# Decode attention over two key-value caches: the transposes of the small cache's first probabilities moved from in front of its second unit to behind that unit's second pair of steps

## The chip, the core and the metric

The kernel runs on one core of one Trainium2 chip. The metric is device time in microseconds (us), lower is better.

Names used below: PE is the tensor engine, PEld its weight load, DVE the vector engine, ACT the scalar engine, SP the sync engine, which only issues the large loads.

## The reference, cut to what matters

Two decode attentions for a single query position, 32 query heads of 128 each, in bf16. Cache A ("large") has 32 key-value heads with all of its 32768 positions in use. Cache B ("small") has 8 key-value heads, each shared by 4 query heads, and only the last 4096 positions count.

```python
q = (x @ wq).reshape(B, Sq, 32, 128).transpose(0, 2, 1, 3)      # x: [1, 1, 512]
scores = einsum("bhqd,bhkd->bhqk", q, k_cache) * 128 ** -0.5   # B: the last 4096 keys only
p = softmax(scores, axis=-1)
o = einsum("bhqk,bhkd->bhqd", p, v_cache)
out = o.transpose(0, 2, 1, 3).reshape(B, Sq, 32 * 128) @ wo    # A's and B's outputs side by side
```

Nearly all of the work is reading: about 570 MB of keys, values and weights.

## The kernel before

The program is a list of operations per engine, in program order, with semaphores placed from the dependencies. The parts that matter (cuts marked `...`):

```python
def plan(self):
    ...
    self.load_wq("B")                        # v buffer 0
    for g in range(2):
        self.load_kv("k", "B", g, 0, 0)      # k buffers 0 and 1
    self.load_wq("A")                        # v buffer 1
    self.emit_qproj("B")
    self.emit_unit("B", 0, 0, 0)             # transposes of K, copies out of PSUM, scores
    self.emit_stats("B", 0, 0)               # max, exponential -> psb
    self.emit_PT("B", 0, 0)                  # transposes of psb -> ptsb
    self.emit_unit("B", 1, 0, 0, lambda: self.emit_qproj("A"))
    self.emit_stats("B", 1, 0)
    for g in range(2):
        if g == 1:
            self.emit_PT("B", g, 0)
        self.load_kv("v", "B", g, 0, 0)      # v buffers 0 and 1
        self.emit_PV("B", g, 0, 0)
        self.emit_gather("B", g, 0)
    ...
    for i in range(self.NIT):                # the large cache: 32 rounds, 4 loads of 4 MB each
        ...

def emit_unit(self, name, g, r, u, late=None):
    slot = u if name == "A" else g
    for pr in range(4):                      # four pairs of steps
        for st in (2 * pr, 2 * pr + 1):
            for half in range(2):
                self.emit_T(slot, st, half)  # 8 transposes into one of 4 PSUM banks, one copy on DVE
        if pr == 3 and late:
            late()                           # the large cache's q projection
        self.pending.append((name, g, r, u, pr, self.nbatch - 4))
        if len(self.pending) > 1:
            self.emit_S(self.pending.pop(0)) # scores of the pair before
```

First, there are two V buffers. The projection weights of the large cache (`wq` of A, 4 MB) sit in V buffer 1, and the small cache's second V load goes into the same buffer. So that load waits until PE has finished the large cache's q projection. Its semaphore comes with the first step of scores (four matmuls) after the projection. Second, SP issues its loads strictly in order, so every load of the large cache queues behind this one. PE in turn reaches the projection only after the last transposes of the second small-cache unit.

## Time and profile before

| | before |
|---|---|
| time, median of 3 runs | 1338.75 us (1337.97 to 1339.37) |
| span in the profile | 1335.2 us |
| PE / DVE busy | 71% / 59% |
| DMA over the span | 427 GB/s |
| second V load of the small cache issued at | 54.59 us |

From the page of the kernel before, part 1 (busy microseconds and share of the span) and part 2 (40 equal slices of the span; busy tenths of the DMA engines, then GB/s):

```profile
span 1335.2 us, 41413 instructions
PE 954.6 (71%) x19416; PEld 771.0 (58%) x19416; DVE 791.1 (59%) x1662; ACT 61.1 (5%) x201; POOL 2.0 (0%) x15
DMA  9999999999999999999999999999999999999998
GB/s 394 377 427 436 426 436 426 438 425 438 426 437 427 436 428 434 430 434 429 435 429 435 428 435 429 435 429 434 430 432 432 432 432 431 432 432 432 431 433 354
```

DMA moves at least 425 GB/s in all slices but three: the first (start), the last (end), and the second (33 to 67 us, 377 GB/s). The second is the one that can be repaired. The view of windows of 1 us shows it closely. Its columns are the window and its length, busy us and instruction count of each engine, the granted PE clock, the DMA share, and GB/s:

```profile
51.00:52.00 1.00, 1.00 (x46) 1.00 (x43) 1.00 (x3) 0.00 (x0) 0.00 (x0) 1.00 0.83 344
52.00:53.00 1.00, 1.00 (x46) 1.00 (x43) 0.23 (x1) 0.00 (x0) 0.00 (x0) 1.00 0.32 123
53.00:54.00 1.00, 1.00 (x46) 1.00 (x43) 0.00 (x0) 0.00 (x0) 0.00 (x0) 1.00 0.08 33
54.00:55.00 1.00, 1.00 (x21) 0.52 (x21) 0.19 (x1) 0.00 (x0) 0.00 (x0) 0.76 0.00 0
55.00:56.00 1.00, 1.00 (x16) 0.40 (x12) 0.24 (x1) 0.00 (x0) 0.00 (x0) 0.50 0.56 66
56.00:57.00 1.00, 1.00 (x16) 0.39 (x12) 0.90 (x4) 0.00 (x0) 0.00 (x0) 0.50 0.56 213
57.00:58.00 1.00, 1.00 (x13) 0.31 (x8) 0.91 (x5) 0.00 (x0) 0.00 (x0) 0.53 1.04 442
```

The last column falls to zero although PE is busy throughout: the load before has landed in full at 54.06 us and the next is not yet issued, so the queue holds nothing. The timeline says why (start, duration, engine, line, operation; in brackets the idle time before it and what ended that):

```profile
36.14 0.69 DVE L511 TENSOR_REDUCE tr_in<-psS 128x1 f32<-128x512 f32 x1 [0.51 <-PE psS L493]
...
39.47 0.69 ACT L525 ACTIVATE psb<-psS,nb_B 128x512 bf16<-128x512 f32 x1 [36.49 <-DVE nb_B L524]
...
40.31 0.61 PE L538 MATMUL psPT<-ident,psb 128*128 128x128 bf16 x4 [4.22 <-ACT psb L525]
40.71 5.45 PE L470 MATMUL psT<-ident,kbuf 128*128 128x128 bf16 x64
41.81 0.69 DVE L473 COPY kt<-psT 128x1024 bf16<-128x1024 bf16 x1 [2.37 <-PE psT L470]
...
50.87 3.34 PE L427 MATMUL psACC<-x_A,vbuf 128*128 128x1 bf16 x128
54.14 1.57 PE L493 MATMUL psS<-kt,qz 128*32 128x512 bf16 x16
...
54.59 0.37 SPq L291 DMA_DIRECT2D vbuf<-in_B_v_cache_dram  x1
```

Read it from the bottom. The V load is issued at 54.59, right after the projection (L427), which is the end of PE's second unit. That unit starts late. PE stands 4.22 us in front of the four transposes of psb (L538), because they need the exponential on ACT, which needs the statistics on DVE. Meanwhile the second unit's K data is there and four PSUM banks are free.

### The profile page before, as it was taken

The page shows a single profiled execution, that of the slowest core. Times are in us where ns is not written, and L with a number is a line of the kernel's source. Part 1 is how long each engine was busy: PE and PEld are TensorE (multiplying, and loading weights), DVE is VectorE, ACT ScalarE, POOL GpSimd, SP SyncE. Part 2 cuts the span into 40 slices and gives each one's busy share as a digit, 9 for nine tenths or more (in the row PEclk, how much of TensorE's full clock was granted, in tenths as well). Part 3 has the DMA queues.
Part 4 walks back from the last instruction along what each step waited for, and adds up shares of the span by engine and source line. Part 5 has one row for each costly group of instructions (what it writes and reads, how often), then busy time and mean ns, then how long its engine had stood idle before and what let it go on. Part 6 is the DMA issues. An engine that isn't in the chain of part 4 may idle for free.

```text
span 1335.2 us, 41413 instructions
## 1 busy us (share of the span) xinstructions
PE 954.6 (71%) x19416; PEld 771.0 (58%) x19416; DVE 791.1 (59%) x1662; ACT 61.1 (5%) x201; POOL 2.0 (0%) x15
## 2 busy tenths in 40 slices
PE   3676766877766787776767777666877766777776
PEld 3455555656655565665556566555655655566663
DVE  3564655676555576655556665555666555666652
ACT  0000000000000000000000000000000000000000
POOL 0000000000000000000000000000000000000000
PEclk9787888888787888887888888788889887888888
DMA  9999999999999999999999999999999999999998
GB/s 394 377 427 436 426 436 426 438 425 438 426 437 427 436 428 434 430 434 429 435 429 435 428 435 429 435 429 434 430 432 432 432 432 431 432 432 432 431 433 354
DMA packets 22003, 570.64 MB, mean 427 GB/s; under 512 B 2530, under 2 KB 2532, under 8 KB 2788
## 3 DMA queue, kind: packets, MB, share of 16 engines
q1 hardware_dynamic: 21700, 570.44, 99.5%
q8 instruction: 10, 0.16, 0.0%
q10 hardware_dynamic: 288, 0.00, 0.0%
q14 instruction: 5, 0.04, 0.0%
HBM read 570.43 MB, written 0.00 MB: 427 GB/s over the span
## 4 chain that ended last, share of the span: by engine, by line
DMA 64%; PE 26%; issue 0%; DVE 0%; SPq 0%
DMA kbuf<-in_A_k_cache_dram 63%; PE psT L470 22%; PE psS L493 4%; DMA kbuf<-in_A_wo_dram 2%; PE psPT L635 0%; DVE out_sb L639 0%; SPq L291 0%
## 5 line engine op out<-in xcount | busy, mean ns | idle before, releaser
L473 DVE COPY kt<-psT 128x1024 bf16<-128x1024 bf16 x1056 | 655.2, 684 | 216.8 <-PE psT L470 214.4
L470 PE MATMUL psT<-ident,kbuf 128*128 128x128 bf16 x8448 | 575.5, 233 | 138.3 <-DMA kbuf<-in_A_k_cache_dram 130.1
L470 PEld LDWEIGHTS psT<-ident,kbuf 128*128 128x128 bf16 x8448 | 536.2, 106 | 230.1 <-DMA kbuf<-in_A_k_cache_dram 138.2
L563 PE MATMUL psACC<-vbuf,ptsb 128*2 128x128 bf16 (+1 forms) x8256 | 188.5, 272 | 45.6 <-ACT ptsb L541 22.0
L563 PEld LDWEIGHTS psACC<-vbuf,ptsb 128*2 128x2 bf16 (+1 forms) x8256 | 169.0, 106 | 67.1 <-ACT ptsb L541 30.5
L493 PE MATMUL psS<-kt,qw 128*32 128x512 bf16 x2048 | 157.7, 385 | 15.2 <-DVE kt L473 15.2
L538 PE MATMUL psPT<-ident,psb 128*128 128x128 bf16 x136 | 20.5, 305 | 135.1 <-ACT psb L525 135.1
L592 DVE SCALAR_TENSOR_TENSOR oc_A<-psACC,hot_A,oc_A 128x128 f32<-128x128 f32 x48 | 16.8, 351 | 144.7 <-PE psACC L563 144.7
L538 PEld LDWEIGHTS psPT<-ident,psb 128*128 128x128 bf16 x136 | 11.6, 130 | 145.0 <-ACT psb L525 144.8
L525 ACT ACTIVATE psb<-psS,nb_A 128x512 bf16<-128x512 f32 x32 | 22.0, 687 | 1174.6 <-DVE nb_A L524 1174.6
L493 PEld LDWEIGHTS psS<-kt,qw 128*32 128x32 bf16 x2048 | 33.9, 95 | 57.7 <-DVE kt L473 31.0
L589 DVE TENSOR_SCALAR oc_A<-psACC,hot_A 128x128 f32<-128x128 f32 x16 | 5.6, 351 | 92.8 <-PE psACC L563 92.8
L511 DVE TENSOR_REDUCE tr_in<-psS 128x1 f32<-128x512 f32 x34 | 23.5, 692 | 18.1 <-PE psS L493 18.1
L606 PE MATMUL psG<-oc_A,hw 128*32 128x128 f32 (+1 forms) x128 | 14.4, 223 | 24.9 <-DVE oc_A L592 19.4
L514 DVE COPY m<-tr_a 1x16 f32<-1x16 f32 (+1 forms) x136 | 22.3, 164 | 2.6
L606 PEld LDWEIGHTS psG<-oc_A,hw 128*32 128x32 f32 x128 | 6.6, 110 | 29.9 <-issue 29.9
L520 DVE COPY b_A<-mr_A 1x16 f32<-1x16 f32 x128 | 21.2, 165 | 2.4
L541 ACT ACTIVATE ptsb<-psPT 128x512 bf16<-128x512 bf16 x34 | 20.3, 597 | 18.5 <-PE psPT L538 18.5
L575 DVE TENSOR_SCALAR oc_A<-oc_A,alpha_A 128x129 f32<-128x129 f32 x16 | 4.6, 290 | 16.4 <-ACT alpha_A L528 16.4
L427 PE MATMUL psACC<-x_B,vbuf 128*128 128x1 bf16 x128 | 3.6, 165 | 13.2 <-DMA vbuf<-in_B_wq_dram 13.2
L427 PEld LDWEIGHTS psACC<-x_B,vbuf 128*128 128x128 bf16 x128 | 3.5, 104 | 13.2 <-issue 13.2
L528 ACT ACTIVATE alpha_A<-cm_A,nb_A 128x1 f32<-128x1 f32 x32 | 9.0, 283 | 0.0
(71 smaller groups left out, 105.9 us busy)
## 6 DMA issues: line engine op xcount, KB each, us to landing
kbuf<-in_A_k_cache_dram SPq DMA_DIRECT2D x64, 4096.0 KB, 28.1
vbuf<-in_A_v_cache_dram SPq DMA_DIRECT2D x64, 4096.0 KB, 29.8
kbuf<-in_B_k_cache_dram SPq DMA_DIRECT2D x2, 4096.0 KB, 27.8
vbuf<-in_B_v_cache_dram SPq DMA_DIRECT2D x2, 4096.0 KB, 19.0
vbuf<-in_B_wq_dram SPq DMA_DIRECT2D x1, 4096.0 KB, 12.4
vbuf<-in_A_wq_dram SPq DMA_DIRECT2D x1, 4096.0 KB, 41.9
kbuf<-in_B_wo_dram SPq DMA_DIRECT2D x2, 2048.0 KB, 25.6
kbuf<-in_A_wo_dram SPq DMA_DIRECT2D x1, 1536.0 KB, 22.2
```

The costliest lines, as they stand in the source:

```text
L470: inst = e.transpose(T[:, 128 * k:128 * k + 128], src[:, DH * tile:DH * tile + DH], self.ident[:, :])
L473: self.copies.append(self.op("dve", lambda v: v.tensor_copy(KT[:, :], T[:, :]), o, to="pe"))
L493: inst = e.matmul(self.S[32 * c:32 * c + 32, :], lhsT=win, rhs=self.kt[(bb + c // 2) % NKT][:, 512 * (c % 2):512 * (c % 2) + 512], start=f ...
L511: o = dve(lambda v: v.reduce_max(tr["in"][:, 0:1], self.S[:, :], axis=AXX), self.sdone, self.k_pool)
L514: x = dve(lambda v, c=c: v.tensor_copy(m4[0:1, W * c:W * c + W], tr["a"][32 * c:32 * c + 1, 0:W]), o)
L520: x = dve(lambda v, c=c: v.tensor_copy(t["b"][32 * c:32 * c + 1, 0:W].rearrange("p (k h) -> p k h", k=KC), t["mr"][0:1, k, :].unsqueeze(1) ...
L525: self.sread = self.op("act", lambda s: s.activation(out=self.psb[:, :], in_=self.S[:, :], func=ACTF.Exp, bias=t["nb"][:, k:k + 1], scale= ...
L538: inst = e.transpose(PT[:, 128 * jj:128 * jj + 128], self.psb[:, 128 * jj:128 * jj + 128], self.ident[:, :])
L541: self.ptread = self.op("act", lambda s: s.activation(out=self.ptsb[:, :], in_=PT[:, 0:512], func=ACTF.Copy), self.psread, to="pe")
L563: inst = e.matmul(acc[32 * c:32 * c + HG, 0:w], lhsT=pt[:, col:col + HG], rhs=vv[:, :, 16 * kc + 4 * c + jj, :], start=(kc == 0 and jj == ...
L592: self.oop = dve(lambda v, src=src, hot=hot: v.scalar_tensor_tensor(out=oc, in0=src, scalar=hot, in1=oc, op0=ALU.mult, op1=ALU.add), pv, b ...
L606: self.gath = self.op("pe", lambda e, c=c, c2=c2: e.matmul(self.G[0:32, c0 + c:c0 + c2], lhsT=win, rhs=t["oc"][:, c:c2], start=False, stop ...
```

## The change

The intent is to give PE work while DVE and ACT prepare the first probabilities. The transposes of psb move behind the second unit's second pair of steps, where psb is ready. The single `late` hook becomes a table of hooks by pair.

```diff
         self.emit_stats("B", 0, 0)
-        self.emit_PT("B", 0, 0)
-        self.emit_unit("B", 1, 0, 0, lambda: self.emit_qproj("A"))
+        self.emit_unit("B", 1, 0, 0, {1: lambda: self.emit_PT("B", 0, 0), 3: lambda: self.emit_qproj("A")})
         self.emit_stats("B", 1, 0)
...
-    def emit_unit(self, name, g, r, u, late=None):
+    def emit_unit(self, name, g, r, u, hooks={}):
...
-            if pr == 3 and late:
-                late()
+            if pr in hooks:
+                hooks[pr]()
```

No instruction is added or removed. On PE, four matmuls change places with 64; the other engines keep their order.

## The prediction

> **What bounds the kernel.** DMA: the page gives 427 GB/s over the span, and the table of 20 us windows a DMA share of 0.99 to 1.03 from 100 us to 1320 us (PE is busy 71%, DVE 59%). A few microseconds on PE or DVE are worth something only where the DMA queue runs dry. Outside start and end, the 1 us windows show that once, from about 52 us (51:52 344 GB/s, 52:53 123, 53:54 33, 54:55 0, 55:56 66, 56:57 213, 57:58 442): against 430 GB/s, 4 to 4.5 us of lost transfer.
>
> **Why there.** SP issues in order. Its second small-cache V load waits for the large cache's q projection, which reads the same buffer (and for the score matmul after it, which carries the semaphore). The timeline has that projection at 50.87 to 54.21 us and the issue at 54.59; the next K loads queue behind it. So the end of the second small-cache unit's transposes on PE, which the projection follows, is on the critical path.
>
> **What the change moves.** No instruction is added or removed; PE's order shows only the four psb transposes moved, from before the second unit's first 64 transposes (8 groups) to after them. Before, PE finished the first unit's scores at 36.1, then waited 4.22 us for the exponential on ACT, which follows the statistics on DVE (36.14 to 39.43). DVE's copies out of PSUM began only at 41.81, the first of them every 0.85 us, bound by PE; later ones every 0.605. Now four transpose groups fill the four free PSUM banks during the statistics (by bytes moved, the K data landed near 34 us). DVE starts copying at 39.43, 2.4 us earlier. The fifth group still waits for the first copy (about 40.2), so PE idles about 2 us.
>
> **Clock.** The windows show the granted clock fall to 0.50 at about 37.5 us and return at about 44.3; transposes then take 107 ns instead of 56 ns. The Trainium skill, "TensorE: Matmul & The Clock Gate", Part 1 (the HAM clock gate), says that the clock halves after an idle window of about 3.4 us and returns after a busy one; the trace agrees roughly. Estimates from these durations: if PE is cold until 44.3 again, the second unit's transposes end near 48.9, 2 us sooner (the copies' 2.4 us less a bubble in which DVE waits for PE); if it stays warm, DVE's cadence rules and they end near 47.4, 3.5 us sooner. The moved transposes cost PE 0.4 us either way; their output is not needed before the V product near 52 us. Central: 2.4 us.
>
> **On the critical path.** All of it: the V load issue moves from 54.6 to about 52.2 us, the DMA gap shrinks from 4 to about 1.5 us, everything behind shifts by as much, and a saturated DMA neither gives it back nor adds to it. The gap caps the gain at about 4.
>
> **Prediction.** 1336.4 us, range 1334.8 to 1338.4. Faster by over 2%: 0.01; within 2%: 0.98; slower: 0.01.
>
> **What would show it.** PE's wait for the exponential gone from the second unit's head, replaced by a wait for DVE of about 2 us; first copy of unit two at 39.4; the large cache's projection ending at 50.7 to 52.2; second V issue 0.4 us later; more GB/s in 52 to 58 us; the loop's K loads all 2 to 3.5 us earlier.
>
> **What would make it wrong.** The large cache's projection weights landing after 47 us; the second K landing after 36; the loop absorbing the shift through slack that I don't see; a colder PE eating the gain; chip variation of 0.5 us hiding it.

## The result and the profile after

| | before | after |
|---|---|---|
| median, first measurement (4 runs each) | 1338.87 us | 1336.07 us (1335.95 to 1337.26) |
| ratio, 95% interval | | 0.9982 (0.9965 to 0.9999) |
| span in the profile | 1335.2 us | 1334.2 us |
| second small-cache V load issued | 54.59 us | 53.28 us |
| PE idle at the head of the second unit | 4.22 us | 2.11 us, after four groups |

The page of the kernel after, the same lines:

```profile
span 1334.2 us, 41413 instructions
PE 956.5 (72%) x19416; PEld 771.4 (58%) x19416; DVE 790.9 (59%) x1662; ACT 61.2 (5%) x201; POOL 2.0 (0%) x15
DMA  9999999999999999999999999999999999999998
GB/s 393 394 424 436 427 435 428 434 430 432 431 433 431 432 431 430 433 431 432 431 432 430 432 433 430 433 431 433 428 434 429 432 432 432 432 430 434 430 433 351
```

Busy times are within 2 us of before. What moved is the second slice, from 377 to 394 GB/s. The windows of 1 us of the kernel after:

```profile
51.00:52.00 1.00, 1.00 (x46) 1.00 (x44) 0.00 (x0) 0.00 (x0) 0.00 (x0) 1.00 0.90 360
52.00:53.00 1.00, 1.00 (x31) 0.74 (x32) 0.19 (x1) 0.00 (x0) 0.00 (x0) 0.67 0.26 107
53.00:54.00 1.00, 1.00 (x16) 0.32 (x8) 0.00 (x0) 0.00 (x0) 0.00 (x0) 0.50 0.06 25
54.00:55.00 1.00, 1.00 (x16) 0.39 (x12) 0.43 (x1) 0.00 (x0) 0.00 (x0) 0.50 0.58 82
55.00:56.00 1.00, 1.00 (x16) 0.39 (x12) 0.89 (x5) 0.00 (x0) 0.00 (x0) 0.63 0.83 328
56.00:57.00 1.00, 0.92 (x20) 0.19 (x8) 0.91 (x5) 0.00 (x0) 0.00 (x0) 1.00 0.98 401
```

The hole starts at the same time and ends earlier. The timeline of the kernel after:

```profile
36.51 1.96 PE L469 MATMUL psT<-ident,kbuf 128*128 128x128 bf16 x32
...
39.85 4.87 DVE L472 COPY kt<-psT 128x1024 bf16<-128x1024 bf16 x8
...
40.58 2.83 PE L469 MATMUL psT<-ident,kbuf 128*128 128x128 bf16 x32 [2.11 <-DVE kt L472]
43.21 0.63 PE L537 MATMUL psPT<-ident,psb 128*128 128x128 bf16 x4
...
45.75 4.92 DVE L472 COPY kt<-psT 128x1024 bf16<-128x1024 bf16 x8 [1.04 <-PE psT L469]
...
49.33 3.35 PE L426 MATMUL psACC<-x_A,vbuf 128*128 128x1 bf16 x128
...
53.28 0.37 SPq L291 DMA_DIRECT2D vbuf<-in_B_v_cache_dram  x1
```

Four groups of transposes now run at 36.51, during the statistics. DVE starts to copy as soon as the statistics are done (39.85 and not 41.81), pauses once for 1.04 us, because PE runs at half clock there (in the profiles of runs 7 to 9 below, at full clock, all sixteen copies follow each other without a pause), and the V load follows the projection as before.

The two profiles differ by 1.0 us, the timed medians by 2.8 us. Most of the mismatch lies in the profiled execution of before: at 1336.93 us it is faster than all 36 timed runs of before and of its copy (1337.24 to 1339.9). A single pair of profiles is a poor measure of a difference of this size.

### The profile page after: what moved, and what is told of

It reads as the page before. It is cut to its first block, busy times and chain, and to the rows that moved or that the text cites. A ratio compares the mean times of both kernels' runs of the same rounds, so it can differ in the third digit from the quotient of the medians.

```text
span 1334.2 us, 41413 instructions
## 1 busy us (share of the span) xinstructions
PE 956.5 (72%) x19416; PEld 771.4 (58%) x19416; DVE 790.9 (59%) x1662; ACT 61.2 (5%) x201; POOL 2.0 (0%) x15
## 4 chain that ended last, share of the span: by engine, by line
DMA 65%; PE 26%; issue 0%; DVE 0%; SPq 0%
DMA kbuf<-in_A_k_cache_dram 63%; PE psT L469 23%; PE psS L492 4%; DMA kbuf<-in_A_wo_dram 2%; PE psPT L634 0%; DVE out_sb L638 0%; SPq L291 0%
```

## The experiments

Theory A: the gain is the earlier issue of the second V load, because only there does the DMA run dry, and what shortens that hole shortens the kernel. Rival B: the gain comes from PE's removed wait itself, or from how the rest of the kernel falls in time, and the V load is incidental. Eleven runs were made, two of them repeats, all with correct results. Each ratio and each median of before is of the same chip and the same rounds. The median of before is 1338.77 in the first four runs, 1339.20 in the next four and 1337.98 in the last three; these three groups ran on three chips. The interval of each ratio is about 0.0014 (1.9 us) either way, and those of neighbouring kernels overlap; where two kernels with a gain are told apart below, it rests on executions that do not overlap.

### 1. Before against itself

No edit.

> The kernel before, submitted as if it were a change: how much two equal kernels differ on one chip. Every theory expects a ratio of 1.000 within 0.0006 (0.8 us), second small-cache V load issued near 54.6 us, a DMA gap of about 4 us around 52 to 58 us. If the ratio is off by more than 0.001, a difference of 2 us means little here.

Measured: 1338.44 us median (1337.26 to 1339.9), ratio 0.9999 (0.9985 to 1.0013). The mean is where it should be. The spread is larger than expected, and its profiled run at 1339.9 us shows one source of it (timeline):

```profile
42.06 0.61 PE L538 MATMUL psPT<-ident,psb 128*128 128x128 bf16 x4 [4.22 <-ACT psb L525]
42.47 6.30 PE L470 MATMUL psT<-ident,kbuf 128*128 128x128 bf16 x64
...
57.20 0.37 SPq L291 DMA_DIRECT2D vbuf<-in_B_v_cache_dram  x1
```

The first unit's last scores began 1.76 us later than in the profile shown before (37.45 and not 35.69), and the 64 transposes took 6.30 and not 5.45 us. More time at half clock made most of both: the first unit's own first 64 transposes took 6.61 and not 5.08 us. The load left at 57.20 and not 54.59, 2.61 us later, and the run was 2.97 us longer. Two executions of one program already behave as theory A says.

### 2. After again

No edit to the changed kernel.

> The changed kernel again, in more rounds, for a tighter interval. Theory A (the second small-cache V load is issued earlier by what PE gains in the second unit, and the saturated DMA passes that on one for one): the first profiles show the issue 1.3 us earlier (53.28 against 54.59), so 1.3 to 2.8 us less time, ratio 0.9979 to 0.9990. Rival B (the time comes from elsewhere, for instance from how the loop falls against the PE clock, and the V load has nothing to do with it): no fixed number, any ratio from 0.997 to 1.001.

Measured: 1335.76 us (1335.59 to 1337.54), ratio 0.9984 (0.9970 to 0.9997), V load at 52.80. By medians the change is worth 3.0 us here and 2.8 in the first measurement; by the ratios, which use means, 2.1 and 2.4 us.

### 3. Probabilities in front as before, projection earlier

```diff
-        self.emit_unit("B", 1, 0, 0, {1: lambda: self.emit_PT("B", 0, 0), 3: lambda: self.emit_qproj("A")})
+        self.emit_PT("B", 0, 0)
+        self.emit_unit("B", 1, 0, 0, {2: lambda: self.emit_qproj("A")})
```

> The transposes of the probabilities stay in front of the second unit, as before, so PE still waits 4.2 us for the exponential; alone the large cache's projection is taken one pair of steps earlier (after the second unit's third group of four transposes), which lets the second V load be issued about 2.4 us earlier, near 52.2. Theory A: as much gain as the change or a little more, 2 to 2.6 us (ratio 0.9981 to 0.9985). Rival B (what counts is that PE's wait for the exponential is gone): no gain, ratio 1.000 within 0.0005.

Measured: 1335.66 us, ratio 0.9981 (0.9968 to 0.9995). From its timeline:

```profile
40.92 0.61 PE L538 MATMUL psPT<-ident,psb 128*128 128x128 bf16 x4 [4.21 <-ACT psb L525]
...
53.37 0.37 SPq L291 DMA_DIRECT2D vbuf<-in_B_v_cache_dram  x1
```

The wait of 4.21 us for the exponential is still there, and the gain is that of the change. Rival B's "no gain" falls: PE's wait costs only through what it delays.

### 4. The change and the earlier projection together

```diff
-        self.emit_unit("B", 1, 0, 0, {1: lambda: self.emit_PT("B", 0, 0), 3: lambda: self.emit_qproj("A")})
+        self.emit_unit("B", 1, 0, 0, {1: lambda: self.emit_PT("B", 0, 0), 2: lambda: self.emit_qproj("A")})
```

> The change and the earlier projection together: V load issued near 50.9 us, before the data queued ahead of it has run out at about 52. Theory A: the gains add up to the size of the gap and no further, 3.5 to 4.2 us under before (ratio 0.9969 to 0.9974), GB/s from 51 to 58 us without a hole under 300. Rival B: the same as the change alone, whatever the V load does.

Measured: 1334.24 us (1334.19 to 1334.39), ratio 0.9969 (0.9955 to 0.9982). V load at 50.28. Windows of this run:

```profile
51.00:52.00 1.00, 1.00 (x22) 1.00 (x19) 0.95 (x2) 0.00 (x0) 0.00 (x0) 1.00 1.13 418
52.00:53.00 1.00, 1.00 (x19) 0.40 (x16) 1.00 (x3) 0.00 (x0) 0.00 (x0) 1.00 0.90 311
53.00:54.00 1.00, 0.51 (x8) 0.10 (x4) 0.53 (x1) 0.00 (x0) 0.00 (x0) 1.00 1.03 434
54.00:55.00 1.00, 0.76 (x16) 0.41 (x20) 0.91 (x2) 0.00 (x0) 0.00 (x0) 1.00 1.01 426
```

The hole is closed, and the gain by medians, 4.5 us, is a little over the expected cap of 4.2. The five executions now lie within 0.20 us, where those of before spread over 1.5 in the same rounds and over 2.6 in run 1. That fits the reading that with the load no longer late the PE clock's changing phase no longer reaches the total. This kernel beats before and after without an added instruction.

### 5 and 6. A buffer of its own for the projection weights, without and with the change

```diff
+        self.wqa = sb("wqa", [128, UT * DH], BF16)
...
+        if name == "A":
+            self.wqasem = self.nc.alloc_semaphore("wqasem")
+            self.load(self.wqa[:, :], src, self.wqasem)
+        else:
+            self.load_slot("v", slot, self.vbuf[slot][:, :], src)
...
-        ps, wq = self.ACC, self.vbuf[slot]
+        ps, wq = self.ACC, self.vbuf[slot] if name == "B" else self.wqa
```

The first of the two keeps the transposes of the probabilities in front, the second has them where the change puts them.

> The projection weights of the large cache get a buffer of their own (32 KB a partition), so the second V load waits for no projection; transposes of the probabilities in front, as before. Theory A: V load issued with the first one near 30 us, no gap, 3.8 to 4.5 us under before (ratio 0.9966 to 0.9972), although PE still waits 4.2 us for the exponential. Rival B (PE's wait costs the time): at most 0.5 us of gain.

> The same buffer, with the change. Theory A: with the V load decoupled the change is worth nothing: equal to the run with the buffer alone within 0.6 us, although PE's second unit ends 1.3 to 2 us earlier. Rival B: the change is worth its 1.3 to 2.8 us here too, on top of the buffer's.

Measured: 1334.37 us without the change (ratio 0.9966, 0.9953 to 0.9980) and 1334.43 us with it (0.9968, 0.9954 to 0.9981). The timelines, first without the change, then with it:

```profile
30.87 0.92 SPq L292 DMA_DIRECT2D vbuf<-in_B_v_cache_dram  x2
...
52.31 3.34 PE L433 MATMUL psACC<-x_A,wqa 128*128 128x1 bf16 x128
```

```profile
30.12 0.92 SPq L292 DMA_DIRECT2D vbuf<-in_B_v_cache_dram  x2
...
48.96 3.39 PE L432 MATMUL psACC<-x_A,wqa 128*128 128x1 bf16 x128
```

Both issue the V load with the first one, at about 31 us. With the change the projection starts at 48.96, without it at 52.31, and the 3.35 us are worth nothing: by medians it is 0.06 us slower, and the executions of the two overlap (1334.17 to 1334.47 and 1334.28 to 1334.97). This is the clearest separation: the same change is worth 2 to 3 us where the load waits for the projection, and nothing where it doesn't.

### 7. The change, with idle PE work ahead of the projection

```diff
-        ... 3: lambda: self.emit_qproj("A")
+        ... 3: lambda: (self.keep_busy(60), self.emit_qproj("A"))   # 60 transposes of the identity into PT, result unused
```

> The change, with 60 idle transposes of the identity (about 3.3 us of PE at full clock, result unused) just ahead of the large cache's projection. PE's wait for the exponential stays away, but the V load is issued near 56.6 us. Theory A: 3.3 us over the change, so 0.5 to 2 us over before (ratio 1.0003 to 1.0016). Rival B (the removed wait on PE is what counts, the DMA absorbs the rest): as the change, under before.

Measured: 1338.76 us (1338.48 to 1340.05), ratio 1.0002 (0.9988 to 1.0016), just under the range expected. PE's wait for the exponential is gone, and so is the gain. The load left at 55.80, earlier than expected, because this execution had full clock throughout. The median is 0.4 us under that of before, where the change's was 3.0 us under (run 2, another chip), so the delay cost about 2.6 us. Its fastest execution, 1338.48, is slower than the slowest of run 2, 1337.54.

### 8. The change, with PE kept busy during the statistics

```diff
-        ... {1: lambda: self.emit_PT("B", 0, 0), 3: lambda: self.emit_qproj("A")}
+        ... {0: lambda: self.keep_busy(36), 1: lambda: self.emit_PT("B", 0, 0), 3: lambda: self.emit_qproj("A")}
```

> The change, with 36 idle transposes of the identity (about 2 us) behind the first four transpose groups, in the time in which PE waits for the first copy anyhow. It asks what the clock costs: in the changed kernel the granted clock is 0.50 from 42.5 to 45.3 us, where PE goes on after 2.1 us of idling. Clock theory: without the idling the clock stays at 1.0, the copies come every 0.605 us without the 1.0 us pause of DVE, the V load is issued 1 to 1.5 us earlier than with the change, and the time falls by as much (ratio to before 0.9968 to 0.9980). If the low clock comes from something other than that idling, nothing changes or the V load comes up to 0.3 us later.

Measured: 1336.23 us median, ratio 0.9974 (0.9960 to 0.9987), but in two groups: 1333.92 and 1334.61, and 1336.23 to 1336.74. The windows of the kernel after, here with the clock (third column from the end) in view:

```profile
40.00:42.00 2.00, 1.42 (x20) 1.12 (x21) 2.00 (x4) 0.93 (x3) 0.00 (x0) 1.00 0.73 311
42.00:44.00 2.00, 2.00 (x24) 1.62 (x25) 2.00 (x4) 0.12 (x1) 0.00 (x0) 0.52 0.97 397
44.00:46.00 2.00, 2.00 (x25) 1.26 (x18) 0.96 (x3) 0.47 (x1) 0.00 (x0) 0.62 1.03 426
```

and of this kernel:

```profile
40.00:42.00 2.00, 1.90 (x32) 1.58 (x30) 1.93 (x6) 0.96 (x3) 0.00 (x0) 1.00 0.74 315
42.00:44.00 2.00, 2.00 (x36) 1.47 (x33) 2.00 (x4) 0.14 (x1) 0.00 (x0) 1.00 1.00 401
44.00:46.00 2.00, 2.00 (x39) 1.70 (x32) 2.00 (x5) 0.46 (x1) 0.00 (x0) 1.00 1.00 414
```

At full clock the projection starts 11.76 us after the first unit's last scores begin, and not 13.15. That is the clock's price, 1.4 us. But the clock was full in runs 7, 9 and 10 too, without such filling there, so this run does not show that the filling kept it (see "The clock" below for run 11). One execution, 1333.92 us, is faster than every execution without a hole (1334.17 at least), and nothing here explains it. The load left at 52.26, and the profiled run was nevertheless 1336.42 us. What cost it that is told below under "Where the ends are decided".

### 9. Probabilities behind the projection

```diff
-        self.emit_unit("B", 1, 0, 0, {1: lambda: self.emit_PT("B", 0, 0), 3: lambda: self.emit_qproj("A")})
+        self.emit_unit("B", 1, 0, 0, {3: lambda: self.emit_qproj("A")})
+        self.emit_PT("B", 0, 0)
```

> The change carried further: the four transposes of the probabilities stand behind the large cache's projection and the scores after it, so they take nothing from the way to the V load. In the changed kernel they cost PE 0.45 to 0.6 us in front of the projection. Theory A (V load issue decides): issue 0.3 to 0.6 us earlier than with the change, time under the change by as much, 1335.2 to 1335.6 us. If what matters is only that they are not in front of the second unit: as the change.

Measured: 1335.74 us (1335.56 to 1337.96), ratio 0.9982 (0.9969 to 0.9996). By the median this is a miss: no better than the change. The load left at 52.07, but in an execution at full clock, so it can't be set beside the change's own trace. It can be set beside runs 7 and 8, at full clock too: with the four transposes in front, PE passes the end of the second unit's transposes 11.75 and 11.76 us after the first unit's last scores begin, here after 11.53. So they hold the load up by 0.2 us at full clock, too little for these times to show. Inconclusive in time.

### 10. A small hole on purpose

```diff
-        ... 3: lambda: self.emit_qproj("A")
+        ... 2: lambda: (self.keep_busy(21), self.emit_qproj("A"))
```

> The change and the projection two steps earlier, with 21 idle transposes (1.2 us) ahead of the projection, so that the V load is issued near 51.5 us and not 50.3. All sixteen shares of the V load before it land at 52.5 us first and at 54.4 last. Theory A1 (every microsecond of issue counts, as the first share sees it): the first share of the second V load lands 1.2 us later and the time rises by as much, to 1335.3 or 1335.5 us. Theory A2 (the end follows the share that lands last, and a gap that only the leading shares see lets the trailing ones catch up): the first share 1.2 us later too, but the last share and the time move by at most 0.4 us, 1334.2 to 1334.6 us.

Measured: 1335.69 us (1334.46 to 1336.81), ratio 0.9983 (0.9969 to 0.9997), V load at 51.61. The median is nearest to what A1 expects (every microsecond counts), but the five executions span both expectations. The profiled run, 1335.12, stands between: the second V load's first and last shares landed 1.25 and 1.23 us later than in run 4, but at the large cache's third K load, near 114 us, the last share was only 0.11 us later; the run was 0.88 us longer. (The landings in the expectation are read on a clock that is 0.3 us ahead of the one of this text.) Inconclusive between A1 and A2.

### 11. Full clock and the earlier projection

```diff
-        ... {1: lambda: self.emit_PT("B", 0, 0), 3: lambda: self.emit_qproj("A")}
+        ... {0: lambda: self.keep_busy(36), 1: lambda: self.emit_PT("B", 0, 0), 2: lambda: self.emit_qproj("A")}
```

> The change, PE kept busy during the statistics, and the projection two steps earlier, so that the V load is issued near 49 us, well before it is needed. Both theories: as the projection two steps earlier alone, 1334.2 us within 0.4: where no gap is left a faster PE is worth nothing.

Measured: 1334.51 us (1334.26 to 1334.69), ratio 0.9973 (0.9960 to 0.9987), V load at 49.44. As expected a floor: no gain from 0.84 us of earlier issue.

### Where the ends are decided

The Trainium skill, "DMA: Bandwidth & Descriptors", section "Why a DMA increments its semaphore by 16 and not by 1", says that a transfer runs on up to 16 engines that finish independently and each add one to its semaphore. The trace agrees: each 4 MB load reports sixteen times. From these records (us from the start of the span, as in the views; first and last of the sixteen shares; the hole is the time between the first share of the two V loads less 9.71 us, the steady distance of loads):

| profiled run | V load issued | hole, first share | last K load, first share | last K load, last share | time of this run |
|---|---|---|---|---|---|
| before | 54.59 | 4.59 | 1290.36 | 1292.39 | 1336.93 |
| 1 before again | 57.20 | 7.26 | 1292.73 | 1295.34 | 1339.90 |
| after | 53.28 | 3.27 | 1288.92 | 1291.40 | 1335.95 |
| 2 after again | 52.80 | 2.89 | 1288.75 | 1290.96 | 1335.61 |
| 3 front, early projection | 53.37 | 3.45 | 1289.19 | 1291.05 | 1335.59 |
| 4 after, early projection | 50.28 | 0.39 | 1286.21 | 1289.70 | 1334.24 |
| 5 own buffer, front | about 31 | 0.21 | 1286.06 | 1289.61 | 1334.28 |
| 6 own buffer, after | about 31 | 0.21 | 1285.96 | 1289.76 | 1334.28 |
| 7 delayed | 55.80 | 5.86 | 1291.73 | 1293.67 | 1338.48 |
| 8 PE kept busy | 52.26 | 2.26 | 1287.95 | 1291.90 | 1336.42 |
| 9 behind the projection | 52.07 | 2.38 | 1288.44 | 1292.93 | 1337.96 |
| 10 small hole | 51.61 | 1.59 | 1287.43 | 1290.43 | 1335.12 |
| 11 kept busy, early projection | 49.44 | 0.21 | 1285.91 | 1289.70 | 1334.26 |

In every row the time is the last share of the last K load plus 44.5 to 45.0 us. The first share keeps nearly the whole hole to the end: before minus run 4 is 4.20 us of hole, and 4.15 us at the last K load. The last share keeps 2.69 us, which is just the difference of the two times (1336.93 less 1334.24). Set against run 4 in the same way, before, after and runs 1, 2, 3 and 7 all have 1.1 to 1.7 us less of time than of hole. Between two executions that both keep a hole this part cancels: run 1 less run 2 is 4.37 us of hole and 4.29 of time, before less after 1.32 and 0.98.

A likely reason can be seen, though no run tested it alone. In the first loads of all traces single shares fall behind, mostly by 1 to 2 us at a time: of the first K load in before, fifteen shares land within 0.45 us and the last 1.68 us after the first. A hole of 2.89 us or more sets nearly all of them level again: of the second V load in before, fifteen land within 0.30 us, and in every trace with such a hole at most one trails by over 1 us, while in run 4, without a hole, six do. So part of what a hole costs seems to be given back, as it waits for stragglers that would have decided the end anyway. The profiled executions of runs 8 and 9 are slower than their V load promised, and they are also those where the hole, 2.26 and 2.38 us, did not buy this: four shares of the second V load trail by over 1 us, and at the large cache's third K load their last share is 3.7 and 4.3 us behind the first, more than in run 4 (3.3), while it is 1.8 and 2.0 us behind in before and after.

## Why the prediction was right

- **DMA bounds the kernel, with one hole near 52 us.** Right. Runs 4, 5, 6 and 11 close the hole and reach the same median of 1334.2 to 1334.5 us by different routes.
- **The second V load waits for the projection, and PE's second unit is on the critical path only through it.** Right, and shown from both sides: earlier issue without the change gains as much (run 3), the change without the dependency gains nothing (run 6 against run 5), the change with a delayed projection gains nothing (run 7).
- **Copies start 2.4 us earlier; PE waits about 2 us for DVE; four transposes cost 0.4 us.** Right: the copies start 1.96 us earlier between the two profiles and 2.45 us earlier reckoned from the start of the first unit's last scores; PE waits 2.11 us; the four transposes take 0.56 us to the next matmul at half clock (0.32 in run 8 at full clock). From the start of the first unit's last scores (35.69 and 36.18) to the issue it was 18.90 us before and 17.10 after, 1.80 us less, against the predicted 2.0 for a cold PE and 3.5 for a warm one.
- **The clock.** The skill's "TensorE: Matmul & The Clock Gate", Part 1, calls the window free-running and the number of cold matmuls run-variable, and the traces agree: in the changed kernel the half clock came at 42.1 to 45.5 us and not at 37.5 to 44.3, and two executions of before took 5.45 and 6.30 us for the same 64 transposes. Four of four profiles with the probabilities in front (4.2 us of idling) have the half clock in the second unit. Of the seven with the change's later place and no filling ahead of the fifth group, which idle 2.1 us there, four have it and runs 7, 9 and 10 do not. The records hold what divides them. In these traces the granted clock changes only on a grid of 3.41 us, which lies differently in each execution (it stays for 3.41, 6.83, 10.24 us and other multiples). Of the grid's windows that begin at full clock between 24 and 42 us, in all thirteen profiles, those with up to 1.31 us of idle PE are followed by full clock and those with 1.90 us or more by half. In runs 7, 9 and 10 a boundary of the grid cuts the 2.1 us of idling into two parts of at most 1.31 us; in the other four, 1.90 to 2.11 us of it lie in one window. In run 11 the idling, if it had come as long after the first unit as in the others (38.46 to 40.57 us, an estimate from their timelines), would have lain in one window too (38.27 to 41.69 us), and with the filling the clock stayed full: there the filling most likely kept it. The prediction's "agrees roughly" is about right: in before the clock fell after a window with 1.95 us of idling, not one that was idle throughout.
- **V load at 52.2 us, 2.4 us earlier.** Off in the trace by 1.1 us (53.28; 52.80 in run 2). Of this, 0.49 us is a first unit that ended later than in the profile of before, which shifts from run to run; the other 0.6 us is that the load gained 1.80 us on its own unit and not the central 2.4. The clock did fall to half, which is the prediction's cold case. Against typical executions of before, which are slower than the one profiled, the size is right.
- **"The gap caps the gain at about 4."** Mis-sized. The gap of the profiled execution was 4.59 us for the first share; in the longest execution seen, it was 7.26. Closing it was worth 4.5 us (run 4) and 4.8 us (run 5) by medians.
- **"A saturated DMA neither gives it back nor adds to it."** Right for the first share, only partly for the last one, which sets the end: 2.69 of 4.20 us in the pair before and run 4. For this change it nearly held, since before and after both keep a hole and what is given back mostly cancels between them.

The time, 1336.07 and 1335.76 us against 1336.4 predicted, was right for the predicted reason. That it came so close was also luck, since the predicted shift was read from an execution of before that was faster than those it was subtracted from.

Open: why single shares fall back by one step at a time (see the last section), and whether a hole of about 1 us costs its full length.

## What to carry to other kernels

In a kernel that saturates DMA, look for the moments at which the queue is empty, and follow the late issue back through the in-order issuing engine to the buffer that it waits for; here, engine idle time that did not delay that load was worth nothing that the times show (run 6 against run 5). Reordering the engine that releases the buffer helps, but moving the release itself forward (run 4), or giving the tenant a buffer of its own (run 5), closes the hole, and the executions then lie within 0.2 to 0.7 us. Take a change of a few tenths of a per cent from several timed runs, and compare in each profile the event that is said to matter, not only the span.

## What the Trainium skill lacked or had wrong

- "Runtime: NRT & Kernel Launch", section "Instruction fetch mechanics", says that instructions come in 16 KiB blocks by DMA and that crossing a block is mostly hidden. The trace of before shows ten such packets of 16384 bytes, 0.97 to 1.09 us each; the profile's page counts them among the traffic of the core's DMA engines. For the engine that waits for instructions they may be hidden. For a saturated load they seem not to be: before has one at 18.64 us, and of the K load whose first share lands at 22.67 us one share is 1.2 us behind the other fifteen; in every load from there to the hole at least one share trails the first by over 1.2 us. That the packets cause it is inferred from the times, not tested, and they are not the whole cause: shares still fall back after the last packet of before (193.51 us), one more by 0.78 us in the load that lands at 309 us.
- No page says that shares that have drifted apart stay so while the queue is full and can be levelled by a hole: in run 4, without a hole, the sixteen shares of the large cache's third K load land over 3.3 us and those of its last over 3.5, in before over 1.8 and 2.0.
- "TensorE: Matmul & The Clock Gate", Part 1, ties the half clock to idle windows. In the kernel after the granted clock falls to 0.67 at 52 to 53 us and to 0.50 at 53 to 54 us, just behind a projection of 128 matmuls with one column each, in windows in which PE counts as fully busy, as it does from 46 us on. The busy time that the profile shows, with its modelled ends of matmuls, is not what the clock follows here. Nor does a page say how much of a window may be idle: here 1.31 us of 3.41 left the clock at full and 1.90 us did not.
